# Attention with routed experts on one core: weighted sum ten steps behind the scores, routing rounds of 24 tiles, key chunks loaded two in turn

## The chip, the cores and the metric

The kernel runs on one core of a Trainium2 chip. The metric is the device time of one execution in microseconds (us); lower is better. A core has five engines with an instruction stream each: TensorE (PE in the profile; its weight loads are PEld), VectorE (DVE), ScalarE (ACT), GpSimd (POOL) and SyncE (SP, which here only issues DMAs). Each stream is executed in order and waits on semaphores. SP and POOL both issue DMAs; POOL also computes.

## The reference

Four batches of pooled attention, then a mixture of experts over all 49,152 output rows:

```python
def _attn_ref(q, kv, w_sr):                       # q (4, 12288, 128), kv (4, 384, 32, 128)
    kv_pool = kv.reshape(B, H // 4, 4, W // 4, 4, C).mean(axis=(2, 4))
    k = v = kv_pool.reshape(B, -1, C) @ w_sr      # 768 keys a batch
    s = (q @ k.transpose(0, 2, 1)) / sqrt(C)
    a = exp(s - s.max(-1)); a /= a.sum(-1) + 1e-09
    return a @ v

def _moe_ref(x, w_skip, w_gate, w1, w2):          # 8 experts, 128 -> 1024 -> 128
    act = x @ w_skip > 0                          # rows that are computed
    e = argmax(x @ w_gate); g = softmax(x @ w_gate)[e]
    out[act] = x + g * (relu(x @ w1[e]) @ w2[e])  # the others keep x
```

## The kernel before

The attention phase works on 384 tiles of 128 queries, 96 to a batch. A loop over steps t writes all engines' streams by hand; a step takes one tile through one stage each of a pipeline. In step t, `scores(t)` issues six 384-column matmuls (query in a high and a low part, keys too), `row_max(t)` reduces them on DVE (L641), `row_exp(t)` is the exponential on ACT (L646). One step later `p_hi` (ACT, L650) and `p_lo` (DVE, L654) split four of the six key chunks of the weights into two f16 parts, which SP sends through a transposing DMA into `pt` (L657). The other two chunks are transposed on PE two steps later (`p_transpose`, L670) and split from PSUM (L678, L679). `attend(t - LAG)` with LAG = 8 is the weighted sum, 18 matmuls of 138 columns (L696). Four tiles form a group; queries come a group at a time (`load_q`, three groups ahead), their high part is cast on ACT (L612), their low part is subtracted on POOL in two halves (L615, `q_lo`), placed in the steps t + 2 and t + 4 after a group's second step, two groups before use.

The keys and values of the next batch arrive during the current one: six chunks of four row sets each. The first row set of a chunk is a plain DMA from SP (L444), the other three are DMAs from POOL that add into the same tile (L446); each must wait until the one before it has landed. `KV_T` places one of the 24 loads every 3.25 steps, chunk after chunk. POOL then folds the chunk (L472, L475) four steps after its last load.

Routing: every RT = 12 tiles, when the last of them is summed, a job `route(r, ...)` starts. It yields between its parts, so that they spread over the next twelve steps: gate logits and maximum on DVE (L741, L743), five elementwise operations on POOL (L745 to L759), one-hot marks (L771 to L774), a scan that ranks the rows of each expert (L779), three tiny matmuls over the partitions (L793 to L795), destinations (L799 to L822), and `send_rows`. That one reads a flag on POOL and, inside a `tc.If`, scatters the rows into a DRAM buffer `scr` with one indirect DMA (L191). The job for round r ends in the step in which that of round r + 1 begins, and stands just ahead of it in POOL's stream.

The last 60 steps also load and split the weights and rows of one expert group whose place is known after three batches. From step 384 on, PE does what is left of the weighted sums interleaved with this first group (`peel`), DVE works out the last round and a table of all groups (`make_table`), and then the expert loop starts: 17 passes over 2,048 rows, bound by PE, which the change doesn't touch.

Of the kernel before, what the change touches and what calls it, by code (L numbers as in the profile page):

```python
# [9 lines left out]
F32 = mybir.dt.float32  # L10
F32R = mybir.dt.float32r
BF16 = mybir.dt.bfloat16
# [8 lines left out]
RT = 12  # L21
# [3 lines left out]
def kernel(  # L25
# [33 lines left out]
    RG = RT // GT  # L59
    TPB = NQ // P  # L60
# [3 lines left out]
    LAG = 8  # L64
    TLAG = 2
    W1, W2, W3 = 3, 6, 0
# [46 lines left out]
    idt_i = consts.tile([P, RT], I32, name="idt_i")  # L113
    nc.gpsimd.iota(idt_i, pattern=[[1, RT]], base=BIG, channel_multiplier=RT)
    idt = consts.tile([P, RT], F32, name="idt")
    nc.gpsimd.tensor_copy(idt, idt_i)

    marks = [consts.tile([P, E, RT + 1], F16, name=f"marks{i}") for i in range(3)]
    for x in marks:
        nc.gpsimd.memset(x, 0.0)  # L120
    keep = consts.tile([P, E, RT + 1], F32, name="keep")
# [282 lines left out]
    with ExitStack() as p1:  # L404
        kprep = p1.enter_context(tc.tile_pool(name="kprep", bufs=1))
        kvm = p1.enter_context(tc.tile_pool(name="kvm", bufs=2))
        qp = p1.enter_context(tc.tile_pool(name="qp", bufs=4))
        qt = p1.enter_context(tc.tile_pool(name="qt", bufs=3))
# [192 lines left out]
        LASTR = NTILE // RT - 1  # L601
        SNAPR = LASTR - 8

# [80 lines left out]
        def attend(t):  # L684
# [23 lines left out]
            def scale():  # L708
# [13 lines left out]
        def route(r, eng):  # L722
            rows = ROWS[r]
            S3 = [P, RT, E]
            x_sc = KV[r * RT // TPB][5]

            def small_t(name, dt=F32):
                return rt.tile([P, RT], dt, name=name)

            def big_t(name, dt=F32):  # L730
                return rt.tile([P, RT, E], dt, name=name)
# [6 lines left out]
            def em(x):  # L738
                return x.unsqueeze(1).broadcast_to(S3)
# [21 lines left out]
            ohb = mark.rearrange("p e t -> p t e")[:, 1:RT + 1, :]  # L761
            yield
            fast = r >= LASTR - 1
# [5 lines left out]
            nc.scalar.copy(rows[:, :, C + 2], x_sc.broadcast_to([P, RT]))  # L769
# [7 lines left out]
            inner = rt.tile([P, E, RT + 1], BF16, name="inner")  # L777
# [4 lines left out]
            nc.vector.tensor_reduce(out=full, in_=inner[:, :, RT], axis=AX.X, op=ALU.max)  # L782
            odd = rt.tile([P, 1], BF16, name="odd")
            nc.vector.scalar_tensor_tensor(out=odd, in0=full, scalar=float(RT), in1=full, op0=ALU.subtract, op1=ALU.mult)
# [8 lines left out]
            nc.tensor.matmul(ps[:, 0:E], upper_bf, inner[:, :, RT], start=True, stop=True)  # L793
            nc.tensor.matmul(ps[:, E:2 * E], ones_bf, inner[:, :, RT], start=True, stop=True)
# [11 lines left out]
            eng.tensor_tensor(out=acc, in0=inner.rearrange("p e t -> p t e")[:, 0:RT, :], in1=em(carry[:, 0, :]), op=ALU.add)  # L806
            eng.tensor_tensor(out=acc, in0=acc, in1=ohb, op=ALU.mult)
            eng.tensor_scalar(out=gs, in0=gs, scalar1=1e-9, scalar2=x_sc, op0=ALU.add, op1=ALU.mult)
            nc.gpsimd.iota(rows.bitcast(I32)[:, :, C + 1], pattern=[[1, RT]], base=r * RT * P, channel_multiplier=RT)
# [4 lines left out]
            if r == SNAPR:  # L814
# [6 lines left out]
            bi = rt.tile([P, 1], I32, name="bi")  # L821
            nc.vector.scalar_tensor_tensor(out=bi, in0=rows.bitcast(I32)[:, 0, C + 1:C + 2], scalar=float(TRASH),  # L822
                                           in1=di[:, 0:1], op0=ALU.add, op1=ALU.min)
            if not few:
                yield
            send_rows(rows, di, bi, mixed)
# [135 lines left out]
        ptq = p1.enter_context(tc.tile_pool(name="ptq", bufs=5))  # L962
        hl = p1.enter_context(tc.tile_pool(name="hl", bufs=6))
# [6 lines left out]
        for i in range(KC * R):  # L970
            KV_T.setdefault(i * 13 // 4, []).append(divmod(i, R))
# [6 lines left out]
        while t < NTILE + LAG - 1 or next_l or jobs:  # L978
# [45 lines left out]
            if t == NTILE:  # L1024
                p_s.close()
                p_kv.close()
                alloc_h(p1.enter_context(tc.tile_pool(name="hp1", bufs=1)))
# [93 lines left out]
```

## Time and profile before

| what | value |
|---|---|
| time, median of 3 runs | 1790.56 us (1790.5 to 1798.45) |
| time of the profiled execution | 1793.98 us |
| its span, first to last instruction | 1792.2 us |
| PE busy | 97% |
| DVE busy | 86% |
| ACT busy | 74% |
| POOL busy | 37% |
| mean granted TensorE clock | 0.996 of full speed |

The busy shares are of the whole span: some 950 us of attention and routing, where four engines work, and some 740 us of the expert loop, where PE is alone the bound. A busy PE need not be at its peak, since a matmul's recorded time covers its passage through the pipeline; the distance from the start of one matmul to the start of the next tells the pace.

### The profile page before, as it was taken

What the parts mean: (1) busy time and instruction counts of PE and PEld (TensorE: products, weight loads), DVE (VectorE), ACT (ScalarE), POOL (GpSimd) and SP (SyncE); (2) the same over time, 40 slices, a digit from 0 to 9 for tenths busy, and PEclk for the clock granted to TensorE, in tenths of its full rate; (3) what the DMA queues carried; (4) which work ended last, traced back from release to release, by engine and by line L of the source; (5) the groups of instructions that cost most, each with busy time, mean ns of one, the idle gap of its engine ahead of it and who ended that gap; (6) DMA issues with size and microseconds to landing.
All of it is one profiled execution on the core that took longest, in us unless ns stands there. A gap on an engine that the chain in (4) does not pass through costs nothing. (4 is left out here: it accounts for less than half of the span.)

```text
span 1792.2 us, 42121 instructions
## 1 busy us (share of the span) xinstructions
PE 1731.6 (97%) x13954; PEld 1248.1 (70%) x13954; DVE 1539.2 (86%) x3405; ACT 1318.1 (74%) x2519; POOL 666.5 (37%) x959
## 2 busy tenths in 40 slices
PE   3999999999999999999999999999999999999997
PEld 2899999989899898999989544444444444444443
DVE  6899999999899898999999778878888887788886
ACT  2888888888888887889899456666666666666664
POOL 3334433443443444233323233333333333333334
PEclk9999999999999999999999999999999999999999
DMA  7999999999999999999999333343333333333333
GB/s 180 193 215 224 219 226 205 217 224 216 218 199 213 221 211 214 187 184 202 241 185 209 102 85 100 98 102 95 95 95 98 102 97 102 97 95 104 99 101 84
DMA packets 609814, 284.84 MB, mean 159 GB/s; under 512 B 495616, under 2 KB 564352, under 8 KB 609664
## 3 DMA queue, kind: packets, MB, share of 16 engines
q1 hardware_dynamic: 588064, 222.76, 63.0%
q0 software_dynamic: 21600, 60.19, 13.0%
q8 instruction: 82, 1.34, 0.3%
q14 instruction: 68, 0.56, 0.1%
HBM read 90.47 MB, written 72.30 MB: 91 GB/s over the span
## 5 line engine op out<-in xcount | busy, mean ns | idle before, releaser
L183 POOL DMA_INDIRECT out_dram<-o,ids x288 | 283.3, 984 | 486.8 <-DVE o L325 419.0
L294 DVE SCALAR_TENSOR_TENSOR h_lo<-h_ps,h_hi 128x512 f16<-128x512 f32 x544 | 343.9, 685 | 134.2 <-ACT h_hi L293 134.2
L646 ACT ACTIVATE p_sb<-s_ps,nm 128x768 f32<-128x768 f32 x384 | 347.3, 905 | 126.5 <-DVE nm L641 123.5
L641 DVE TENSOR_REDUCE nm<-s_ps 128x1 f32<-128x768 f32 x384 | 364.7, 950 | 34.0 <-PE s_ps L635 32.4
L293 ACT ACTIVATE h_hi<-h_ps 128x512 f16<-128x512 f32 x544 | 317.9, 597 | 46.9 <-PE h_ps L292 27.3
L696 PE MATMUL acc_ps<-v_hi,pt 128*128 128x138 f16 x3072 | 320.9, 224 | 0.8 <-DVE rs L704 0.7
L696 PEld LDWEIGHTS <-pt 128*128 128x128 f16 x4608 | 275.9, 97 | 62.0 <-issue 60.3
L696 PE MATMUL acc_ps<-v_lo,pt 128*128 128x138 f16 x1536 | 293.5, 223 | 0.0
L633 PE MATMUL s_ps<-k_hi,q_hi 128*128 128x384 f32 x768 | 292.3, 381 | 0.0
L654 DVE SCALAR_TENSOR_TENSOR p<-p_sb,p 128x512 f16<-128x512 f32 x384 | 282.8, 736 | 3.9 <-ACT p L650 3.9
L635 PE MATMUL s_ps<-k_hi,q_lo 128*128 128x384 f32 x768 | 260.5, 339 | 8.1 <-POOL q_lo L615 8.1
L634 PE MATMUL s_ps<-k_lo,q_hi 128*128 128x384 f32 x768 | 260.8, 340 | 0.0
L650 ACT ACTIVATE p<-p_sb 128x512 f16<-128x512 f32 x384 | 243.3, 634 | 3.6 <-DMA pt<-p 0.8
L615 POOL TENSOR_TENSOR q_lo<-q_sb,q_hi 128x256 fp32r<-128x256 f32 (+1 forms) x190 | 154.2, 820 | 186.2 <-DVE p L654 115.7
L290 PE MATMUL h_ps<-xT,w_hi 128*128 128x512 f16 x544 | 206.2, 379 | 2.5 <-issue 2.5
L306 PEld LDWEIGHTS <-w_hi 128*128 128x128 f16 x1152 | 112.7, 98 | 134.2 <-issue 0.8
L306 PE MATMUL y_ps<-h_hi,w_hi 128*128 128x512 f16 x544 | 206.2, 379 | 0.0
L306 PE MATMUL y_ps<-h_hi,w_lo 128*128 128x512 f16 x544 | 206.2, 379 | 0.0
L291 PE MATMUL h_ps<-xT,w_hi 128*128 128x512 f16 x544 | 206.2, 379 | 0.0
L292 PE MATMUL h_ps<-xT,w_lo 128*128 128x512 f16 x544 | 206.2, 379 | 0.0
L309 ACT ACTIVATE yT<-y_ps,y_sc 128x512 f32<-128x512 f32 x68 | 46.7, 687 | 214.7 <-PE y_ps L306 155.7
L306 PE MATMUL y_ps<-h_lo,w_hi 128*128 128x512 f16 x544 | 195.1, 379 | 0.0
(214 smaller groups left out, 3039.7 us busy)
## 6 DMA issues: line engine op xcount, KB each, us to landing
q_sb<-in_q_dram SPq DMA_DIRECT2D x96, 256.0 KB
out_dram<-rows SPq DMA_DIRECT2D x96, 256.0 KB
xin<-scr SPq DMA_DIRECT2D x75, 276.0 KB
w_raw<-in_moe_w_dram SPq DMA_DIRECT2D x34, 512.0 KB, 3.4
kvt<-in_kv_dram POOLq DMA_DIRECT2D x54, 256.0 KB
kvt<-in_kv_dram SPq DMA_DIRECT2D x42, 256.0 KB
pt<-p SPq DMA_TRANSPOSE x384
out_dram<-o,ids POOLq DMA_INDIRECT x288, 3.6
```

Source lines behind the costliest of these rows:

```text
L183: ins = nc.gpsimd.indirect_dma_start(out=dst, out_offset=bass.IndirectOffsetOnAxis(ap=ids, axis=0), in_=src, in_offset=None, bounds_check= ...
L293: nc.scalar.activation(out=h["hi"][:, c, :], in_=ps, func=AF.Relu)
L294: nc.vector.scalar_tensor_tensor(out=h["lo"][:, c, :], in0=ps, scalar=0.0, in1=h["hi"][:, c, :], op0=ALU.max, op1=ALU.subtract)
L306: nc.tensor.matmul(ps, w[:, c, :], h[x][:, c, :], start=(i == 0), stop=(i == len(terms) - 1))
L633: nc.tensor.matmul(s[:, h, :HK], q_hi, k_hi[:, sl], start=True, stop=False)
L634: nc.tensor.matmul(s[:, h, :HK], q_hi, k_lo[:, sl], start=False, stop=False)
L635: nc.tensor.matmul(s[:, h, :HK], q_lo, k_hi[:, sl], start=False, stop=True)
L641: nc.vector.tensor_reduce(out=NM[t], in_=S_PS[t][:, :, :HK], axis=AX.XY, op=ALU.max, negate=True)
L646: nc.scalar.activation(out=P_SB[t], in_=S_PS.pop(t)[:, :, :HK], func=AF.Exp, bias=NM.pop(t))
L650: nc.scalar.activation(out=P16[t][:, 0, :], in_=p_flat(t)[:, 0:KD * P], func=AF.Copy, scale=2.0 ** PEXP)
L654: LO[:] = [nc.vector.scalar_tensor_tensor(out=p16[:, 1, :], in0=p_flat(t)[:, 0:KD * P], scalar=2.0 ** PEXP, in1=p16[:, 0, :], op0=ALU.mult ...
L696: nc.tensor.matmul(ps[:, j % 2, :], w, v[a][:, k, :], start=(i == 0), stop=(i == len(AVL) - 1))
```

## The change

Five edits, made together:

- LAG goes from 8 to 10: `attend` works on the tile ten steps back. The buffers between (`pt`, `ptq`, and `hl` for the split weights, 6 to 9) grow with it.
- Routing rounds hold NB = 2 blocks of 12 tiles, so RQ = 24. All tiles of `route` are twice as wide, there are 16 rounds and not 32, and each round sends its two blocks separately, six steps apart. In the last round they go back to back. `rowp` and `rt` have two buffers and not three.
- `KV_T` pairs the chunks: the first row set of chunk a, then of chunk b, then the second of a, the second of b, and so on. The 24 loads keep their steps.
- Queries load four groups ahead and not three.
- The pooled chunks and their transposed copy lie in the expert weights' raw buffers `w1_raw` and `w2_raw`, which are first loaded later. This frees room.

```diff
-    LAG = 8
+    NB = 2
+    RQ = NB * RT
+    LAG = 10
+    QA = 4
...
-        rt = p1.enter_context(tc.tile_pool(name="rt", bufs=3))
+        rt = p1.enter_context(tc.tile_pool(name="rt", bufs=2))
...
-                pooled[b] = kprep.tile([P, KC, C], F32, name="pooled")
+                pooled[b] = w1_raw[:, 0:NK].rearrange("p (k c) -> p k c", c=C)
...
-                KVT[b] = kprep.tile([P, NK], F32, name="pT")
+                KVT[b] = w2_raw.rearrange("p k c -> p (k c)")[:, 0:NK]
...
-        LASTR = NTILE // RT - 1
-        SNAPR = LASTR - 8
+        LASTR = NTILE // RQ - 1
+        SNAPR = LASTR - 4
...
-                if o == 0:
-                    ROWS[r] = rowp.tile([P, RT, XW], F32, name="rows")
-            rows = ROWS[r][:, o * GT:(o + 1) * GT, :]
+                if o == 0 and r % NB == 0:
+                    ROWS[r // NB] = rowp.tile([P, RQ, XW], F32, name="rows", bufs=2)
+            at = r % NB * RT + o * GT
+            rows = ROWS[r // NB][:, at:at + GT, :]
...
-                if o == RG - 1:
-                    jobs.append([route(r, nc.vector if r == LASTR else nc.gpsimd), None])
+                if o == RG - 1 and r % NB == NB - 1:
+                    jobs.append([route(r // NB, nc.vector if r // NB == LASTR else nc.gpsimd), None])
...
-            S3 = [P, RT, E]
+            S3 = [P, RQ, E]
...
-            fast = r >= LASTR - 1
+            fast = few
...
-            send_rows(rows, di, bi, mixed)
+            for h in range(NB):
+                part = slice(h * RT, (h + 1) * RT)
+                send_rows(rows[:, part, :], di[:, part], bi[:, h:h + 1], mixed)
+                if h < NB - 1 and not few:
+                    for _ in range(6):
+                        yield
...
-        ptq = p1.enter_context(tc.tile_pool(name="ptq", bufs=5))
-        hl = p1.enter_context(tc.tile_pool(name="hl", bufs=6))
+        ptq = p1.enter_context(tc.tile_pool(name="ptq", bufs=6))
+        hl = p1.enter_context(tc.tile_pool(name="hl", bufs=9))
...
         for i in range(KC * R):
-            KV_T.setdefault(i * 13 // 4, []).append(divmod(i, R))
+            two, at = divmod(i, 2 * R)
+            KV_T.setdefault(i * 13 // 4, []).append((2 * two + at % 2, at // 2))
...
-                if t % GT == 0 and t // GT + RG < NGRP:
-                    load_q(t // GT + RG)
+                if t % GT == 0:
+                    for g in range(3 if t == 0 else t // GT + QA, min(t // GT + QA + 1, NGRP)):
+                        load_q(g)
```

Place one is POOL's stream where a block of rows is sent in the attention phase. Before, the scatter (`scr<-rows,bi`; the twelve single scatters behind it are the branch not taken) is followed at once by the five operations of the next round:

```order
L1117 ISA
L191 DMA scr<-rows,bi 460800x138
L190 ISA
L190 UNCONDITIONAL_BRANCH
L183 DMA scr<-rows,di 460800x138 x12
L190 UNCONDITIONAL_BRANCH
L745 TENSOR_TENSOR d<-lg,mx 128x96
L756 TENSOR_SCALAR ev<-d 128x96
L757 TENSOR_TENSOR ev<-ev,em_80 128x96
L758 TENSOR_SCALAR act<-rows 128x12
L759 TENSOR_SCALAR na<-act 128x12
L615 TENSOR_TENSOR q_lo<-q_sb,q_hi 128x256 x2
```

After the change (line numbers are a few higher) the same place, a round's second block:

```order
L1131 ISA
L194 DMA scr<-rows,bi 460800x138
L193 ISA
L193 UNCONDITIONAL_BRANCH
L186 DMA scr<-rows,di 460800x138 x12
L193 UNCONDITIONAL_BRANCH
L619 TENSOR_TENSOR q_lo<-q_sb,q_hi 128x256 x2
L450 DMA kvt<-in_kv_dram 128x1x512
L750 TENSOR_TENSOR d<-lg,mx 128x192
```

The query halves now stand directly behind the scatter, and the next round's operations, twice as wide, come four steps later.

Place two is POOL's stream during the accumulation of key chunks, with buffer numbers kept, since they tell the chunks apart. Before, one chunk (`kvt_790`) has its three adding loads in a row:

```order
L446 DMA kvt_790<-in_kv_dram 128x1x512
L615 TENSOR_TENSOR q_lo_793<-q_sb_571,q_hi_792 128x256
L615 TENSOR_TENSOR q_lo_969<-q_sb_745,q_hi_968 128x256
L446 DMA kvt_790<-in_kv_dram 128x1x512
L745 TENSOR_TENSOR d_1104<-lg_1100,mx_1102 128x96
L756 TENSOR_SCALAR ev_1106<-d_1104 128x96
L757 TENSOR_TENSOR ev_1106<-ev_1106,em8_80 128x96
L758 TENSOR_SCALAR act_1107<-rows_561 128x12
L759 TENSOR_SCALAR na_1108<-act_1107 128x12
L615 TENSOR_TENSOR q_lo_969<-q_sb_745,q_hi_968 128x256
L446 DMA kvt_790<-in_kv_dram 128x1x512
```

After, two chunks (`kvt_356` and `kvt_443`) alternate:

```order
L450 DMA kvt_356<-in_kv_dram 128x1x512
L619 TENSOR_TENSOR q_lo_750<-q_sb_464,q_hi_749 128x256
L450 DMA kvt_443<-in_kv_dram 128x1x512
L619 TENSOR_TENSOR q_lo_750<-q_sb_464,q_hi_749 128x256
L619 TENSOR_TENSOR q_lo_923<-q_sb_552,q_hi_922 128x256
L450 DMA kvt_356<-in_kv_dram 128x1x512
L619 TENSOR_TENSOR q_lo_923<-q_sb_552,q_hi_922 128x256
L450 DMA kvt_443<-in_kv_dram 128x1x512
```

Between two loads into the same chunk there are now six or seven steps, where there were three or four.

Place three is DVE's stream in the last routing round, beside the first expert group (`h_lo` is that group's second operand, `o` its output). Before:

```order
L325 SCALAR_TENSOR_TENSOR o<-acc_ps,xin_135 128x128 x4
L741 TENSOR_TENSOR lg<-rows,gate_ds 128x96
L743 TENSOR_REDUCE mx<-lg 128x12
L745 TENSOR_TENSOR d<-lg,mx 128x96
L751 SCALAR_TENSOR_TENSOR ev<-d,em_80 128x96
L752 TENSOR_SCALAR act<-rows 128x12
L753 SCALAR_TENSOR_TENSOR na<-rows,idt 128x12
L294 SCALAR_TENSOR_TENSOR h_lo<-up_ps,h_hi 128x512 x2
L771 TENSOR_REDUCE mn<-ev 128x12
L773 TENSOR_TENSOR oh<-em_80,mn 128x96
L774 TENSOR_TENSOR marks_89<-oh,act 128x12x8
L294 SCALAR_TENSOR_TENSOR h_lo<-up_ps,h_hi 128x512 x2
```

After:

```order
L297 SCALAR_TENSOR_TENSOR h_lo<-up_ps,h_hi 128x512 x2
L746 TENSOR_TENSOR lg<-rows,gate_ds 128x192
L748 TENSOR_REDUCE mx<-lg 128x24
L750 TENSOR_TENSOR d<-lg,mx 128x192
L756 SCALAR_TENSOR_TENSOR ev<-d,em_80 128x192
L757 TENSOR_SCALAR act<-rows 128x24
L758 SCALAR_TENSOR_TENSOR na<-rows,idt 128x24
L776 TENSOR_REDUCE mn<-ev 128x24
L778 TENSOR_TENSOR oh<-em_80,mn 128x192
L779 TENSOR_TENSOR marks_88<-oh,act 128x24x8
L784 SCALAR_TENSOR_TENSOR inner<-keep,marks_88 128x200
L787 TENSOR_REDUCE full<-inner 128x1
```

The round's operations now follow each other without the group's operations in between, since PE is in a part of the group that makes no `h_lo`; on PE the three routing matmuls now stand behind a whole second half of the group (24 matmuls into the output and 12 of the next) after the last weighted sum, and the table comes later in the group.

## Rows read from the trace of the kernel before

**Rows 1.** Windows view, attention phase: time, busy time of each engine (instructions), clock
```profile
50.00:350.00 300.00, 297.62 (x3235) 276.42 (x3236) 274.66 (x569) 257.77 (x484) 121.20 (x201) 1.00 1.14 215
```

**Rows 2.** Timeline of PE: first score matmul of tiles two apart
```profile
301.19 0.42 PE L633 MATMUL s_ps<-k_hi,q_hi 128*128 128x384 f32 x1
...
305.94 0.42 PE L633 MATMUL s_ps<-k_hi,q_hi 128*128 128x384 f32 x1
```

**Rows 3.** Timeline of ACT: exponentials of tile 8 and of tile 383
```profile
54.70 0.90 ACT L646 ACTIVATE p_sb<-s_ps,nm 128x768 f32<-128x768 f32 x1 [0.44 <-DVE nm L641]
...
985.29 0.90 ACT L646 ACTIVATE p_sb<-s_ps,nm 128x768 f32<-128x768 f32 x1
```

**Rows 4.** Groups by form, 50 to 1000 us: largest of the preparation's matmuls, busy us
```profile
L558 PE MATMUL acc_ps<-wv,pT 128*128 128x138 f32 x36 | 5.6, 292 | 0.4 <-DVE rs L704 0.2
```

**Rows 5.** View of waits, 50 to 1000 us: total us, times, longest
```profile
POOL kvt L446 <- DMA kvt<-in_kv_dram: 72.4, 18, 6.3
...
DVE mn L771 <- POOL ev L757: 13.4, 7, 4.5
...
PEld acc_ps L670 <- ACT p_sb L646: 9.5, 24, 0.9
PEld s_ps L635 <- POOL q_lo L615: 9.3, 4, 3.7
...
ACT q_hi L612 <- DMA q_sb<-in_q_dram: 5.3, 5, 2.1
```

**Rows 6.** Timeline of POOL around the longest of those waits of PE
```profile
682.77 0.86 POOL L446 DMA_DIRECT2D kvt<-in_kv_dram  x1 [4.85 <-DVE nm L641]
685.00 1.09 POOL L191 DMA_INDIRECT scr<-rows,bi  x1 [1.37 <-DVE rs L704]
690.35 0.34 POOL L745 TENSOR_TENSOR d<-lg,mx 128x96 f32<-128x96 f32 x1 [4.27 <-DMA kvt<-in_kv_dram]
```

**Rows 7.** Timeline of PE and windows view at the same place
```profile
693.07 0.69 PE L635 MATMUL s_ps<-k_hi,q_lo 128*128 128x384 f32 x1 [3.40 <-POOL q_lo L615]
...
693.20:696.20 3.00, 3.00 (x19) 2.69 (x20) 2.96 (x6) 2.47 (x5) 2.46 (x4) 0.50 1.11 248
```

**Rows 8.** Timeline of POOL: a scatter with no key load in flight
```profile
978.84 1.58 POOL L191 DMA_INDIRECT scr<-rows,bi  x1 [4.27 <-DVE bi L822]
980.45 0.36 POOL L745 TENSOR_TENSOR d<-lg,mx 128x96 f32<-128x96 f32 x1
```

**Rows 9.** Instructions of line 190 on POOL's sequencer: ns least/median/most
```profile
L190 POOLq EVENT_SEMAPHORE  x96: 42/43/3068, 113.2 to 1018.3; - x96
```

**Rows 10.** Groups by form of DVE, 50 to 1000 us: busy us, mean ns
```profile
L641 DVE TENSOR_REDUCE nm<-s_ps 128x1 f32<-128x768 f32 x378 | 359.0, 950 | 33.9 <-PE s_ps L635 32.4 <-issue 0.2
...
L779 DVE TENSOR_TENSOR_SCAN inner<-keep,marks 128x104 bf16<-128x104 f32 x31 | 13.2, 427 | 1.5 <-POOL marks L774 1.5
...
L743 DVE TENSOR_REDUCE mx<-lg 128x12 f32<-128x96 f32 x31 | 7.8, 253 | 1.1
...
L802 DVE TENSOR_SCALAR mixed<-acc_ps 1x1 int32<-1x1 f32 x31 | 4.2, 136 | 0.0
```

**Rows 11.** Instructions of line 654 on DVE: ns least/median/most
```profile
L654 DVE SCALAR_TENSOR_TENSOR p<-p_sb,p x384: 670/690/2225, 39.5 to 987.2; 128x512 f16<-128x512 f32 x192
```

**Rows 12.** Timeline of PE: two steps before the first weighted sum
```profile
50.02 0.44 PE L670 MATMUL acc_ps<-ident,p_sb 128*128 128x128 f32 x2 [0.30 <-ACT p_sb L646]
...
51.85 0.33 PE L670 MATMUL acc_ps<-ident,p_sb 128*128 128x128 f32 x1 [0.33 <-ACT p_sb L646]
```

**Rows 13.** Timeline of PE: waits between the last scores and the expert loop
```profile
1014.92 0.18 PE L793 MATMUL acc_ps<-inner,upper_bf 128*128 128x8 bf16 x1 [1.80 <-DVE inner L779]
...
1029.09 0.38 PE L306 MATMUL acc_ps<-h_lo,w_hi 128*128 128x512 f16 x1 [0.49 <-DVE h_lo L294]
1030.97 0.58 PE L306 MATMUL acc_ps<-h_lo,w_hi 128*128 128x512 f16 x1 [1.50 <-DVE h_lo L294]
```

More of the change, by code (lines that the diff above doesn't have):

```diff
@@ L112 @@
                             op0=ALU.mult, op1=ALU.add)
-    idt_i = consts.tile([P, RT], I32, name="idt_i")
-    nc.gpsimd.iota(idt_i, pattern=[[1, RT]], base=BIG, channel_multiplier=RT)
-    idt = consts.tile([P, RT], F32, name="idt")
+    idt_i = consts.tile([P, RQ], I32, name="idt_i")
+    nc.gpsimd.iota(idt_i, pattern=[[1, RQ]], base=BIG, channel_multiplier=RQ)
+    idt = consts.tile([P, RQ], F32, name="idt")
     nc.gpsimd.tensor_copy(idt, idt_i)
-    marks = [consts.tile([P, E, RT + 1], F16, name=f"marks{i}") for i in range(3)]
+    marks = [consts.tile([P, E, RQ + 1], F16, name=f"marks{i}") for i in range(3)]
     for x in marks:
         nc.gpsimd.memset(x, 0.0)
-    keep = consts.tile([P, E, RT + 1], F32, name="keep")
+    keep = consts.tile([P, E, RQ + 1], F32, name="keep")
     nc.gpsimd.memset(keep, 1.0)
@@ L768, in route @@
             nc.scalar.activation(out=ex, in_=d, func=AF.Exp)
-            nc.scalar.copy(rows[:, :, C + 2], x_sc.broadcast_to([P, RT]))
+            nc.scalar.copy(rows[:, :, C + 2], x_sc.broadcast_to([P, RQ]))
             mn = small_t("mn")
@@ L776, in route @@
                 yield
-            inner = rt.tile([P, E, RT + 1], BF16, name="inner")
+            inner = rt.tile([P, E, RQ + 1], BF16, name="inner")
             flat = "p e t -> p (e t)"
@@ L781, in route @@
             full = rt.tile([P, 1], F32, name="full")
-            nc.vector.tensor_reduce(out=full, in_=inner[:, :, RT], axis=AX.X, op=ALU.max)
+            nc.vector.tensor_reduce(out=full, in_=inner[:, :, RQ], axis=AX.X, op=ALU.max)
             odd = rt.tile([P, 1], BF16, name="odd")
-            nc.vector.scalar_tensor_tensor(out=odd, in0=full, scalar=float(RT), in1=full, op0=ALU.subtract, op1=ALU.mult)
+            nc.vector.scalar_tensor_tensor(out=odd, in0=full, scalar=float(RQ), in1=full, op0=ALU.subtract, op1=ALU.mult)
             gs = small_t("gs")
@@ L792, in route @@
             ps = misc_ps()
-            nc.tensor.matmul(ps[:, 0:E], upper_bf, inner[:, :, RT], start=True, stop=True)
-            nc.tensor.matmul(ps[:, E:2 * E], ones_bf, inner[:, :, RT], start=True, stop=True)
+            nc.tensor.matmul(ps[:, 0:E], upper_bf, inner[:, :, RQ], start=True, stop=True)
+            nc.tensor.matmul(ps[:, E:2 * E], ones_bf, inner[:, :, RQ], start=True, stop=True)
             nc.tensor.matmul(ps[:, 2 * E:2 * E + 1], ones_bf, odd, start=True, stop=True)
@@ L805, in route @@
             acc = big_t("acc")
-            eng.tensor_tensor(out=acc, in0=inner.rearrange("p e t -> p t e")[:, 0:RT, :], in1=em(carry[:, 0, :]), op=ALU.add)
+            eng.tensor_tensor(out=acc, in0=inner.rearrange("p e t -> p t e")[:, 0:RQ, :], in1=em(carry[:, 0, :]), op=ALU.add)
             eng.tensor_tensor(out=acc, in0=acc, in1=ohb, op=ALU.mult)
             eng.tensor_scalar(out=gs, in0=gs, scalar1=1e-9, scalar2=x_sc, op0=ALU.add, op1=ALU.mult)
-            nc.gpsimd.iota(rows.bitcast(I32)[:, :, C + 1], pattern=[[1, RT]], base=r * RT * P, channel_multiplier=RT)
+            nc.gpsimd.iota(rows.bitcast(I32)[:, :, C + 1].rearrange("p (b t) -> p b t", b=NB),
+                           pattern=[[RT * P, NB], [1, RT]], base=r * RQ * P, channel_multiplier=RT)
             yield
@@ L820, in route @@
             nc.vector.tensor_tensor(out=di, in0=dest, in1=na, op=ALU.add)
-            bi = rt.tile([P, 1], I32, name="bi")
-            nc.vector.scalar_tensor_tensor(out=bi, in0=rows.bitcast(I32)[:, 0, C + 1:C + 2], scalar=float(TRASH),
-                                           in1=di[:, 0:1], op0=ALU.add, op1=ALU.min)
+            bi = rt.tile([P, NB], I32, name="bi")
+            nc.vector.scalar_tensor_tensor(out=bi, in0=rows.bitcast(I32)[:, 0:RQ:RT, C + 1], scalar=float(TRASH),
+                                           in1=di[:, 0:RQ:RT], op0=ALU.add, op1=ALU.min)
             if not few:
                 yield
-            send_rows(rows, di, bi, mixed)
+            for h in range(NB):
[4 more added lines that the diff above has]
+                        yield
             if r == SNAPR:
@@ L1026 @@
                 p_kv.close()
+                p_q.close()
                 alloc_h(p1.enter_context(tc.tile_pool(name="hp1", bufs=1)))
```

13 lines of the change are left out of this document (7 added, 6 removed).

## The prediction

> **What bounds the kernel now.** The windows view of the attention phase comes first: in 300 us PE is busy for 297.6, but DVE for 274.7 and ACT for 257.8 too [rows 1]. So PE leads, and DVE is close behind; what costs time are the moments in which PE waits for one of the others. How much that is in all follows from the pace. In a quiet stretch two tiles take 305.94 - 301.19 = 4.75 us on PE, 2.375 a tile [rows 2]. From tile 8 to tile 383 ACT's exponentials go from 54.70 to 985.29, 930.6 us for 375 tiles [rows 3]; at the quiet pace they would need 890.6. The excess is 40 us. Not all of it is waiting: the keys and values of three batches are prepared on PE, and the largest of four kinds of matmuls for it is 5.6 us [rows 4], so that all together are 6 to 22, and three small matmuls stand in each routing round. Some 15 to 30 us of stalls are left, and that is the ceiling for this phase. The expert loop behind it is untouched.
>
> The view of waits names two causes, read on PEld, since a matmul that waits first holds up its weight load: 9.3 us in 4 times for `q_lo` from POOL, and 9.5 us in 24 times for the exponentials of ACT [rows 5]. The first has a clear story in POOL's timeline. At 682.77 POOL issues an adding load, then the scatter at 685.00, and it gets to the next round's first operation only at 690.35, released by the load's landing [rows 6]: 7.6 us from the load. On POOL's sequencer the waits around the scatter's branch are mostly 43 ns, but up to 3068 [rows 9], and with no load in flight POOL is through in 980.45 - 978.84 = 1.6 us [rows 8]. So the end of that branch waits for key loads still in flight. Then came five routing operations, then `q_lo`, and PE stood for 3.40 us; the clock granted after that was 0.50, that is 1.2 GHz and not 2.4 [rows 7].
>
> **The change, part by part.**
>
> *Key chunks in turn.* The load ahead of the scatter was itself late: 18 times, one for each chunk of three batches, an adding load waited for the one before it, 72.4 us in all and up to 6.3 [rows 5]. Two loads into one chunk now stand six or seven steps apart (14 us and more at 2.375) and not three or four (7 to 9.5). A load needs less than the 7.6 us of [rows 6], so it has landed. Then POOL reaches scatters on time, and behind the scatter stands `q_lo` at once. Loads and scatters still meet in one step twice a batch (steps 6 and 48, from the 3.25-step grid and the rounds' start). There POOL is held for 7.6 us, 3.2 steps, and a half of `q_lo` that is placed one step behind is needed five steps behind; about one step is left over. I take -9 us; bounds -9.3, and +4 if each of the six meetings cost 0.7, a quarter of the cover that I count on.
>
> *The clock.* The stretch at half clock behind the 3.40 us wait gave 19 matmuls in 3 us [rows 7]; half of its length was lost. It goes with the wait: -1.5 us; bounds 0 and -2.
>
> *Rounds of 24 on DVE.* Fourteen DVE operations a round, from 427 to 136 ns, make 3.36 us in 12 tiles. Twice the width costs little: 96 elements take 253 ns and 768 take 950, a slope of 1.04 ns an element [rows 10]; seven operations are 96 elements wide, so a round of 24 costs 3.36 + 7 x 0.10 and 0.1 more for the scan, 4.2 us, where two of before cost 6.7. That frees 2.5 us of DVE in 24 tiles, 39 us in the phase, 4% of an engine 92% busy. It isn't a gain by itself, since PE leads; it shortens the lag that makes exponentials late. Two other sources of the lag go: DVE waited 13.4 us for POOL's `ev`, behind the scatter [rows 5], which now has four free steps ahead of it; and ACT waited 5.3 us for queries [rows 5], which now come one group (9.5 us) sooner. Against the 9.5 us of [rows 5] I take -7; bounds 0 and -9.5.
>
> *Rounds of 24 on PE and POOL.* Fifteen sets of three small matmuls fewer in the phase, and short waits that no row names one by one: -3 us out of the unnamed rest of the 15 to 30; bounds 0 and -6. Scatters stay 32, and so do their branches. POOL's operations get longer, but are half as many; POOL is busy 121 of 300 us [rows 1].
>
> *LAG 10.* The weighted sums don't wait for their transposed weights before, so the longer lag saves nothing there. It costs at the start: two more steps without a weighted sum. Such a step takes 51.85 - 50.02 = 1.83 us with 0.30 to 0.33 idle by the record [rows 12]; its matmuls alone are 2.375 less 18 of some 0.06, 1.3 us. Two steps lose 0.6 to 1.1 us, and the sums moved to the end are paid in full there: +1.
>
> *The end.* Before, PE waited 1.80 us for the last round and 0.49 + 1.50 for `h_lo` behind the table [rows 13]. After, 36 matmuls stand between the last weighted sum and the routing matmuls; they are recorded at 0.38 us and overlap [rows 13], so that 36 make 6.8 us even at half of that, and DVE's chain of eleven operations of 0.25 to 0.45 is done in 5. That wait goes, -2. But the table now comes later in the group, with fifteen of its operations ahead of one `h_lo`; +2. I take 0; bounds -4 and +4.
>
> *Buffers in the weights' place, two `rows` buffers.* The weights are first loaded 34 steps after the last use of the keys there: nothing. `rows` is the first rival below.
>
> Sum: -9 - 1.5 - 7 - 3 + 1 + 0 = -19.5 us. All gains at their bound: -9.3 - 2 - 9.5 - 6 + 0.6 - 4 = -30. The profiled execution took 1793.98 us, its span 1792.2; the median of the runs is 1790.56, 3.4 less. The profiled time would be 1774.5, and the median 1771.
>
> **The rivals.**
>
> *Slower: `rows` is reused too soon.* With two buffers of 24 tiles, the second scatter of a round is placed six steps ahead of ACT's first write into the same buffer; before it was 26. Six steps are 14.2 us. If POOL reaches the scatter late and the transfer lasts long, ACT waits, and the exponentials behind it. It decides once scatter and landing need more than 14.2 us from that step; POOL's hold of 7.6 us [rows 6] plus a transfer like it would be 15. Each of 14 rounds would then lose a step or so, 14 x 2.4 = 33 us, less the gains of 19.5: 1804. Against it: the second scatter waits for nothing of DVE that isn't long done, and only that of step 6, three times in all, meets a load. Chance 0.07.
>
> *Same: PE's own pace.* If the late exponentials come from the even and odd steps of the pipeline itself and not from routing, the relief on DVE stays unused, and longer single operations (0.35 for 0.25 us) push ACT as often as before. Then only the wait for `q_lo`, the clock, and +1 count, and a part of -9 comes back as waits for ACT: -5 us, 1785. The 24 waits on ACT, nearly one for each of 31 rounds, speak for routing as the cause. Chance 0.17.
>
> *Longer POOL operations hold up DVE.* Line 654 takes 690 ns mostly and 2225 at most [rows 11], the long ones while POOL computes. POOL's routing operations nearly double; if each collision costs twice as much, the relief on DVE is eaten, -7 becomes about 0 or +2, and the time 1779. By the Trainium skill (SBUF — State Buffer, "Who interferes with whom") the second of a VectorE instruction with two SBUF inputs and a GpSimd instruction that reads SBUF blocks until the first has ended, so a longer operation blocks longer; the 2225 ns of line 654 agree. Chance 0.10.
>
> *The change doesn't do what it says.* If the adding loads wait for their turn in the queue and not for the landing of the one before, the turn-taking is void and the wait for `q_lo` stays: -19.5 + 10.5 = -9, 1781.5. The row names the landing as what ended the waits. Chance 0.06.
>
> **How the numbers follow.** The forecast has 0.60: 1771, by its own bounds 1761 to 1780. A measurement here tells 0.5% from no change, 9 us, so faster means below 1781.6. The forecast, the collisions and half of the void turn-taking lie below: 0.60 + 0.10 + 0.03 = 0.73. Within 0.5%: 0.17 + 0.03 = 0.20. Slower: 0.07. The range leaves out the slower rival and the tail of the forecast: 1760 to 1787.
>
> **What the profile would show.** Right: the wait of POOL's adding loads falls from 72.4 us to under 20, PE's wait for `q_lo` from 9.3 to under 2, no half clock inside the attention phase; DVE's routing rows number 15 with 4.2 us a round; PE's wait for exponentials is under 4 us; tile 383's exponential comes 18 to 20 us sooner. Wrong: ACT waits for a scatter's landing ahead of its write into `rows`; PE waits for `q_lo` behind steps 6 and 48; PE waits for ACT as often as before though DVE is less busy; or the expert loop starts later than the attention phase's gain allows.

## The result, and the profile after

| | before | changed | ratio [95% interval] |
|---|---|---|---|
| first comparison, median of 6 and 6 runs | 1793.18 us | 1772.44 us (1770.70 to 1778.48) | 0.9866 [0.9833, 0.9899] |
| the same kernel again, on another chip, 26 and 6 runs | 1799.62 us | 1782.01 us (1774.99 to 1785.26) | 0.9910 [0.9874, 0.9945] |
| profiled execution, span | 1792.2 us | 1776.7 us | |

The changed kernel is faster by 0.9 to 1.3% by the two ratios, and by 21 and 18 us by the medians; 19.5 was forecast. The second comparison was made beside the last experiments. The two ratios differ by 0.0044, 8 us, so a variant within that of the changed kernel isn't told apart from it below. The execution profiled first (1778.48 us) was the slowest of its six.

The gain lies where it was expected, in the attention phase. The timeline of ACT after the change, exponentials of tile 8 and tile 383:

```profile
54.59 0.90 ACT L650 ACTIVATE p_sb<-s_ps,nm 128x768 f32<-128x768 f32 x1 [0.44 <-DVE nm L645]
...
966.23 0.90 ACT L650 ACTIVATE p_sb<-s_ps,nm 128x768 f32<-128x768 f32 x1 [0.31 <-DVE nm L645]
```

Against [rows 3] tile 383 is 985.29 - 966.23 = 19.06 us sooner, and tile 8 stands where it stood. What follows tile 383 takes 3.6 us more (1776.7 - 966.2 = 810.5, before 1792.2 - 985.3 = 806.9). In the changed kernel's second profile the same instruction stands at

```profile
960.91 0.90 ACT L650 ACTIVATE p_sb<-s_ps,nm 128x768 f32<-128x768 f32 x1 [0.31 <-DVE nm L645]
```

5.3 us sooner still, though tile 8 stands 1.7 us later there (56.29). So one profile places this mark within some 5 us; the experiments' differences of that size mean nothing by themselves.

Nor does this mark alone say when the expert loop starts. PE's first matmul of the loop, in the first and in the second profile of the changed kernel:

```profile
1028.32 0.58 PE L293 MATMUL h_ps<-xT,w_hi 128*128 128x512 f16 x1 [2.68 <-issue]
...
1028.61 0.59 PE L293 MATMUL h_ps<-xT,w_hi 128*128 128x512 f16 x1 [8.24 <-issue]
```

The second profile gained 5.3 us up to the mark and lost them again ahead of the loop, where PE stood 8.24 us (2.49 in the kernel before). What holds the loop's start there no row tells.

The windows view of the stretch of [rows 1] (time, then PE, PEld, DVE, ACT, POOL busy with their instructions, clock, DMA share, GB/s):

```profile
50.00:350.00 300.00, 297.20 (x3224) 275.90 (x3225) 264.32 (x504) 260.96 (x480) 109.92 (x153) 1.00 1.17 216
```

DVE is 10.3 us less busy in 300 us and POOL 11.3, while PE remains as full as it was. Why DVE is freed is read from the groups by form, 50 to 1000 us (busy us, mean ns of one, idle before):

```profile
L658 DVE SCALAR_TENSOR_TENSOR p<-p_sb,p 128x512 f16<-128x512 f32 x379 | 270.3, 713 | 3.0 <-ACT p L654 2.7 <-ACT p_sb L650 0.3
...
L784 DVE TENSOR_TENSOR_SCAN inner<-keep,marks 128x200 bf16<-128x200 f32 x16 | 9.1, 568 | 0.0
...
L748 DVE TENSOR_REDUCE mx<-lg 128x24 f32<-128x192 f32 x16 | 5.6, 353 | 0.5
...
L807 DVE TENSOR_SCALAR mixed<-acc_ps 1x1 int32<-1x1 f32 x15 | 2.0, 136 | 0.0
```

`mx` went from 253 to 353 ns at twice the width, the scan from 427 to 568, a scalar operation stayed at 136 [rows 10]. The fourteen means of a round add up to 4.08 us, where 4.2 was forecast. The split of the weights (L658) takes 713 ns on the mean; before it was 279.4 us over 379 operations, 737 ns.

The view of waits, 50 to 1000 us (who waited on whom: total us, times, longest), against [rows 5]:

```profile
POOL kvt L450 <- DMA kvt<-in_kv_dram: 31.6, 8, 10.7
...
POOL scr L194 <- DMA kvt<-in_kv_dram: 15.8, 10, 2.3
...
PEld L700 <- DMA pt<-p: 9.5, 21, 1.9
...
PEld acc_ps L674 <- ACT p_sb L650: 7.4, 14, 1.0
ACT p L654 <- DMA pt<-p: 7.3, 6, 1.8
```

The adding loads wait 31.6 us and not 72.4 (23.1 in the second profile). PE's wait for `q_lo` is gone, and so are DVE's for `ev` and ACT's for queries. What is new is the third row: PE waits for `pt`, the weights that come back through SP's transposing DMA, and ACT too waits for it, to have a buffer free.

How that wait arises is seen in the timeline of SP's sequencer (start, duration of the issue; a row with x3 runs from the first issue's start to the third's end):

```profile
436.53 1.24 SPq L661 DMA_TRANSPOSE pt<-p  x1
...
438.49 7.53 SPq L661 DMA_TRANSPOSE pt<-p  x3
...
450.93 10.20 SPq L661 DMA_TRANSPOSE pt<-p  x3
```

and, 5 us behind the last of these, in PE's:

```profile
456.37 0.29 PE L700 MATMUL acc_ps<-v_hi,pt 128*128 128x138 f16 x2 [1.60 <-DMA pt<-p]
```

The first issue takes 1.24 us. The three from 438.49 on take 1.29, 4.56 and 1.47, the three from 450.93 on 3.40, 3.38 and 3.21, where key loads (issued by POOL at 438.12 and 447.48) and scatters (441.23 and 453.97) are in flight, so that SP falls behind its steps of 2.4 us. By the Trainium skill (DMA: Bandwidth & Descriptors, "Queues, rings and completion order") each DMA engine goes round-robin between the queue rows with work, a packet at a time; that a transpose is slower while POOL's transfers run agrees with these rows, though they show its issue and not its packets.

A late SP also holds up POOL. SP issues the first row set of a chunk (L448), and POOL's first adding load waits for it; here are SP's rows and then POOL's:

```profile
397.26 8.36 SPq L661 DMA_TRANSPOSE pt<-p  x3
...
406.34 0.60 SPq L448 DMA_DIRECT2D kvt<-in_kv_dram  x1
...
412.67 0.99 POOL L450 DMA_DIRECT2D kvt<-in_kv_dram  x1 [10.72 <-DMA kvt<-in_kv_dram]
```

All eight waits that make up the 31.6 us are of this kind: each ends with the landing of a load that SP issued, none with that of another adding load. Before, too, 11 of the 18 waits, 44.7 of the 72.4 us, ended with a load of SP's.

### The profile page after: what moved, and what is told of

Read it like the earlier page. It is cut to its first block, busy times and chain, and to the rows that moved or that the text cites. A ratio compares the mean times of both kernels' runs of the same rounds, so it can differ in the third digit from the quotient of the medians.

```text
span 1776.7 us, 41426 instructions
## 1 busy us (share of the span) xinstructions
PE 1721.4 (97%) x13906; PEld 1240.2 (70%) x13906; DVE 1502.7 (85%) x3181; ACT 1317.0 (74%) x2487; POOL 632.0 (36%) x799
## 3 DMA queue, kind: packets, MB, share of 16 engines
q0 software_dynamic: 21600, 60.19, 12.9%
## 5 line engine op out<-in xcount | busy, mean ns | idle before, releaser
L658 DVE SCALAR_TENSOR_TENSOR p<-p_sb,p 128x512 f16<-128x512 f32 x384 | 273.7, 713 | 3.0 <-ACT p L654 2.7
L619 POOL TENSOR_TENSOR q_lo<-q_sb,q_hi 128x256 fp32r<-128x256 f32 (+1 forms) x190 | 147.8, 779 | 327.2 <-DVE p L658 195.6
```

Source lines behind the costliest of these rows:

```text
L658: LO[:] = [nc.vector.scalar_tensor_tensor(out=p16[:, 1, :], in0=p_flat(t)[:, 0:KD * P], scalar=2.0 ** PEXP, in1=p16[:, 0, :], op0=ALU.mult ...
```

## The experiments

All ratios are to the kernel before, run beside it on the same chip, with their 95% intervals. "PE stands" means the sum, over PE's matmuls of the phase, of what the distance from one start to the next has over the median distance of that kind of pair; for the kernel before it gives 10.5 us at `q_lo` and 8.2 us ahead of the transposes by PE, where the exponentials are waited for. The changed kernel has 6.4 for `pt` and 4.6 for the exponentials.

**Key chunks in turn, alone.** The kernel before with only the new `KV_T`:

```diff
-            KV_T.setdefault(i * 13 // 4, []).append(divmod(i, R))
+            two, at = divmod(i, 2 * R)
+            KV_T.setdefault(i * 13 // 4, []).append((2 * two + at % 2, at // 2))
```

> The kernel before with the key chunks two in turn and nothing else changed. Theory (turn-taking alone ends the wait for q_lo and the half clock that follows it): PE's wait for q_lo falls from 9.3 to under 2 us and the time falls by 9 to 11 us, to about 1783 (0.994). Rival (the scatter and the five operations behind it hold up the query halves whatever the loads do): PE's wait for q_lo stays above 5 us and the time stays at 1790 to 1793 (0.998 to 1.000).

Measured: 1798.77 us, 1.0025 [0.9994, 1.0056]. No gain. The view of waits, 50 to 1000 us:

```profile
ACT q_hi L612 <- DMA q_sb<-in_q_dram: 22.8, 17, 3.4
PEld acc_ps L670 <- ACT p_sb L646: 17.2, 24, 2.8
ACT p L650 <- DMA pt<-p: 16.7, 9, 4.6
...
PEld L696 <- DMA pt<-p: 5.8, 5, 2.8
```

Neither the adding loads' wait nor PE's for `q_lo` has a row any more, so the edit does what the prediction said, and yet nothing is won: ACT waits 22.8 us for queries (5.3 before) and 16.7 for the buffers of its split weights, and PE waits for ACT 17.2 us where it was 9.5. The stall changed its place.

**Chunks in a row again.** The changed kernel with the old `KV_T`, `divmod(i, R)`:

> The changed kernel with the key chunks loaded one after the other, as before. Theory (turn-taking ends the late adding loads, which held up the scatter and the query halves): POOL's wait of adding loads on the landing of the one before goes back to about 70 us, PE's wait for q_lo back to 5 us or more, and the time rises by 5 to 11 us, to about 1780 (0.992). Rival (the wait for q_lo went since the next round's operations no longer stand behind the scatter): PE's wait for q_lo stays under 2 us and the time stays at about 1772.

Measured: 1779.00 us, 0.9897 [0.9860, 0.9934], not told apart from the changed kernel. Its waits:

```profile
POOL kvt L450 <- DMA kvt<-in_kv_dram: 128.6, 31, 9.0
...
PEld acc_ps L674 <- ACT p_sb L650: 17.5, 21, 2.9
...
ACT rows L716 <- DMA scr<-rows,bi: 3.6, 1, 3.6
...
PEld s_ps L639 <- POOL q_lo L619: 0.2, 1, 0.2
```

The adding loads wait 128.6 us, more than ever, and PE still doesn't wait for `q_lo`. So the late loads are not enough for that stall: in the kernel before, five routing operations stood between the scatter and `q_lo`; here `q_lo` stands directly behind the scatter. The third row is the first rival's wait, a write into `rows` held by a scatter: once, 3.6 us.

**LAG 10 alone.** The kernel before with the longer lag and buffers for it:

```diff
-    LAG = 8
+    LAG = 10
...
-        ptq = p1.enter_context(tc.tile_pool(name="ptq", bufs=5))
-        hl = p1.enter_context(tc.tile_pool(name="hl", bufs=6))
+        ptq = p1.enter_context(tc.tile_pool(name="ptq", bufs=6))
+        hl = p1.enter_context(tc.tile_pool(name="hl", bufs=8))
```

> The kernel before with the weighted sum ten steps behind and the buffers that go with it (6 for the PE-transposed chunks, 8 for the split weights), no other edit. Theory (before, PE hardly waits for transposed weights; it does so only where POOL and DVE no longer slow the phase down, so the lag is worth something only together with the other edits): the time stays within 0.3% of before, ratio 0.998 to 1.002, PE's wait for q_lo stays near 9 us. Rival (the lag by itself is worth the 15 us that the changed kernel lost with eight): ratio about 0.992.

Measured: 1793.78 us, 0.9974 [0.9946, 1.0002]: at most half a per cent. Its waits:

```profile
POOL kvt L446 <- DMA kvt<-in_kv_dram: 101.2, 27, 7.2
...
PEld acc_ps L670 <- ACT p_sb L646: 16.3, 22, 2.6
```

No row of PE names `q_lo`. A round starts when its last tile is summed, so LAG moves every scatter by two steps against loads and queries; in this profile all but two of the scatters are followed by `q_lo`. So the stall at `q_lo` needed two things, a late load and the five operations between scatter and `q_lo`: the chunks in turn take away the first, the wide rounds and LAG 10 the second. Here too PE waits for ACT instead, 16.3 us for 9.5.

**LAG 8 in the changed kernel.**

```diff
-    LAG = 10
+    LAG = 8
```

> The changed kernel with the weighted sum eight steps behind and not ten, all else as changed. Theory (the lag saves nothing by itself and costs 1 us at the start): the time stays within 0.3% of the changed kernel, about 1771 us (ratio to before 0.986), and PE waits for transposed weights about as much as with ten, 5 to 10 us. Rival (SP's queue falls behind when a key load and a scatter meet, and the two extra steps of lag cover that): PE's waits for transposed weights rise by 10 us or more, and the time to about 1780 us (0.992).

Measured: 1788.45 us, 0.9951 [0.9922, 0.9979]; against the changed kernel that is 7 to 15 us, by which of its two comparisons one takes. Its waits:

```profile
PEld L700 <- DMA pt<-p: 19.8, 15, 3.6
PE acc_ps L700 <- DMA pt<-p: 15.1, 12, 3.3
...
PEld acc_ps L674 <- ACT p_sb L650: 3.7, 8, 1.1
```

PE stands 18.6 us for `pt`, and waits only 3.7 for ACT. So the two steps are cover: with ten, the transposed weights are late by 6.4 us in one profile and by nothing that can be told in the other (no single wait above 0.2); with eight, by 18.6.

**Queries three groups ahead in the changed kernel.**

```diff
-    QA = 4
+    QA = 3
```

> The changed kernel with queries loaded three groups ahead, as before, and not four. Theory (with turn-taking alone ACT waited 22.8 us for queries, since DMAs land later; the group ahead covers that): ACT's wait for queries comes back with 5 us or more, and the time rises by 2 to 6 us (ratio 0.988 to 0.990). Rival (the other edits cover it): no wait of ACT for queries, and the time stays at 0.9866.

Measured: 1787.02 us, 0.9947 [0.9915, 0.9979], 7 to 14 us above the changed kernel. Its waits:

```profile
ACT q_hi L616 <- DMA q_sb<-in_q_dram: 35.3, 26, 3.8
...
PEld acc_ps L674 <- ACT p_sb L650: 21.7, 25, 2.6
```

ACT waits 26 times for queries, as often as PE then waits for ACT: 25 times, 19.5 us by PE's starts. A late query is a late exponential.

**Queries four ahead, alone.** The kernel before with that edit and a fifth query buffer:

```diff
-                if t % GT == 0 and t // GT + RG < NGRP:
-                    load_q(t // GT + RG)
+                if t % GT == 0:
+                    for g in range(3 if t == 0 else t // GT + 4, min(t // GT + 5, NGRP)):
+                        load_q(g)
```

> The kernel before with queries four groups ahead and not three, and nothing else. If queries pay by themselves, ACT's wait for queries (5.3 us before) goes to 0 and the ratio is 0.992 to 0.996. If they pay only where something else has moved the DMAs into their way, as with three groups in the changed kernel (35 us of waits), nothing is gained: ratio 0.998 to 1.002, and PE keeps its wait of about 10 us for q_lo.

Measured: 1797.87 us, 0.9980 [0.9949, 1.0011]. ACT's wait for queries is gone, and the time stays. Its waits:

```profile
PEld s_ps L635 <- POOL q_lo L615: 11.4, 5, 5.7
...
PEld acc_ps L670 <- ACT p_sb L646: 5.6, 16, 0.9
```

PE waits less for ACT (5.6 for 9.5), and as long as before for `q_lo`, to which nothing was done.

**The cover alone.** The changed kernel with rounds of 12 and chunks in a row; what is left is LAG 10, queries four ahead, nine split-weight buffers:

```diff
-    NB = 2
+    NB = 1
...
-        SNAPR = LASTR - 4
+        SNAPR = LASTR - 8
...
-            two, at = divmod(i, 2 * R)
-            KV_T.setdefault(i * 13 // 4, []).append((2 * two + at % 2, at // 2))
+            KV_T.setdefault(i * 13 // 4, []).append(divmod(i, R))
```

(`rt` and `rows` have three buffers again.)

> The changed kernel without its two edits that were meant to help POOL and DVE: key chunks in a row as before, rounds of 12. What is left is LAG 10, queries four groups ahead, and nine buffers for the split weights. If the gain comes from cover for late DMAs, most of it stays: 1775 to 1784 us (ratio 0.988 to 0.993), and PE waits for exponentials and transposed weights stay under 20 us together. If chunks in turn and wide rounds are what gives the gain, as the prediction had it (16.5 of 19.5 us), the time goes back to about 1790 to 1797 (ratio 0.995 to 1.0), with an adding-load wait of POOL above 70 us and a wait of PE for q_lo.

Measured: 1793.04 us, 0.9976 [0.9949, 1.0002]. The first expectation falls: cover alone gives half a per cent at most. Its waits:

```profile
POOL kvt L450 <- DMA kvt<-in_kv_dram: 108.4, 27, 8.0
...
PEld acc_ps L674 <- ACT p_sb L650: 16.2, 20, 3.4
...
PEld L700 <- DMA pt<-p: 3.2, 20, 0.2
```

The second expectation named the time rightly, but not by its wait: of `q_lo` PE has one wait of 0.7 us; it waits for ACT.

**Rounds of 12 in the changed kernel.** As above, but with the chunks in turn:

> The changed kernel with routing rounds of 12 tiles (32 rounds, three buffers of rows and of the routing tiles), all else as changed. Theory (half the rounds free about 39 us of DVE, which is what ended the late exponentials): DVE is busy some 30 to 40 us more between 50 and 1000 us, PE waits for exponentials about 9 us again, and the time is 7 to 10 us above the changed kernel, about 1780 (0.992). Rival (DVE's slack is enough either way): the time stays within 3 us of the changed kernel.

Measured: 1782.94 us, 0.9913 [0.9882, 0.9944]. Beside the cover alone this adds the chunks in turn: 0.9976 becomes 0.9913. Beside the changed kernel it lacks the wide rounds, which are worth 0 to 8 us by the two comparisons. Its waits:

```profile
PEld L700 <- DMA pt<-p: 11.2, 26, 1.4
...
PEld acc_ps L674 <- ACT p_sb L650: 8.1, 15, 1.4
```

DVE is busy for 867.3 us between 50 and 1000 us, against 845.5 in the changed kernel: 22 us more, where 30 to 40 were expected. And PE waits 8.1 us for the exponentials, against 7.4 and 6.4 in the two profiles of the changed kernel: hardly more, though the routing takes DVE twice as many rounds.

**Six split-weight buffers in the changed kernel** (`hl` 9 to 6):

> The changed kernel with six buffers for the split weights and not nine. Theory (these buffers come free when the transposing DMA has read them; turn-taking alone made ACT wait 16.7 us for that): ACT's wait for transposing DMAs rises from 7 to 15 us or more, PE waits for exponentials more, and the time rises by 3 to 8 us (0.988 to 0.991). Rival (six are enough at this pace): time within 2 us of the changed kernel.

Measured: 1780.40 us, 0.9899 [0.9865, 0.9932], not told apart. The wait that the buffers cover is there all the same:

```profile
ACT p L654 <- DMA pt<-p: 34.5, 27, 3.8
...
PEld acc_ps L674 <- ACT p_sb L650: 15.1, 21, 2.1
```

**Loads moved out of the scatters' steps.** The changed kernel with another grid:

```diff
-            KV_T.setdefault(i * 13 // 4, []).append((2 * two + at % 2, at // 2))
+            KV_T.setdefault(24 * two + (2, 7, 9, 11, 14, 16, 18, 20)[at], []).append((2 * two + at % 2, at // 2))
```

> The changed kernel with the 24 key loads of a batch on steps that keep clear of the scatters (eight per 24 steps, none in a scatter's step or the two ahead of it), still two chunks in turn. Theory (transposed weights are late where key loads and scatters are in flight together, around 445 to 460 us in the changed kernel): PE's and ACT's waits for transposing DMAs fall from 17 to under 6 us together, POOL no longer waits for a key load at a scatter, and the time falls by 3 to 6 us (0.983 to 0.985). Rival (the transposes are late by their own number, whatever POOL's DMAs do): waits for transposing DMAs stay above 10 us and the time stays at 0.9866.

Measured: 1772.04 us, 0.9849 [0.9811, 0.9888], within the intervals of the changed kernel. No scatter has a key load within 8 us ahead of it any more, where the first profile of the changed kernel has twelve (counted in POOL's timeline). Its waits:

```profile
POOL kvt L450 <- DMA kvt<-in_kv_dram: 53.8, 19, 6.7
...
PEld L700 <- DMA pt<-p: 13.5, 20, 2.3
...
ACT p L654 <- DMA pt<-p: 8.3, 8, 1.7
```

The theory expected the waits of PE and ACT for transposes to fall from 17 to under 6 us; they are 21.8. So its rival came out: the transposes are late though no load and scatter meet, and the time stays. Two things weaken the comparison. The profile is of the slowest of this kernel's seven executions (1785.85 us). And the new grid puts loads into one chunk four to seven steps apart and not six or seven, so that adding loads wait for each other again (10 of the 19 waits). POOL is held less behind its scatters, and PE doesn't gain by it.

**The same with queries five groups ahead** (QA 5, `hl` 8):

> The changed kernel with the loads' steps moved off those of the scatters, queries five groups ahead and eight buffers for split weights. If queries are still late now and then, another 2 to 5 us are gained over the changed kernel: 1767 to 1770, ratio 0.983 to 0.985. If four groups are enough, the time is that of the run with the loads moved alone, ratio 0.985 to 0.987, or a little above for the buffer that is missing.

Measured: 1785.77 us, 0.9934 [0.9901, 0.9968]. No further gain; it may even cost something, for which its waits give only a part (ACT for `pt` 18.3 us in 11 times, PE for ACT 11.7).

**The changed kernel again.**

> The changed kernel once more, beside the others of this call: ratio 0.984 to 0.989. Its profile tells how far tile 383's exponential (966.2 us in the first profile) and the single waits move from one execution to the next: by under 3 us if the differences between the other profiles are to be read at face value, by 5 us and more if not.

Measured: 1782.01 us, 0.9910 [0.9874, 0.9945], the second line of the first table; its mark is 5.3 us off that of the first profile. PE's wait for `pt` is 1.7 us in 11 times, against 9.5 us in 21.

## Why the prediction was right, and which steps were not

The time, 1771, came out, in the phase that was forecast and with most of the waits that were to go. That the sum came out so closely is luck in part: of its terms, one was set at nothing that wasn't, two were smaller than forecast, and over a quarter of the gain between the marks has no name. PE's time between the two exponentials, added up by line from the starts of its matmuls (a wait counts with the line ahead of it), went from 930.6 to 911.6 us: scores 439.1 to 431.8, weighted sums 421.4 to 413.1, transposes 54.9 to 53.6, routing matmuls 3.2 to 1.2. Term by term:

- **Wait for `q_lo`:** -10.5 by the starts, -9 forecast. The wait went. But the step that gave the whole of it to the chunks in turn was wrong: it goes too with chunks in a row and wider rounds (adding loads waiting 128.6 us), and with LAG 10 alone (101.2 us), where something else stands between scatter and `q_lo`. "An adding load waited for the one before it" was read too narrowly: 11 of the 18 waits were for SP's plain load. Of such waits 31.6 and 23.1 us remain, over the 20 that were named as a sign. And the step that the wait's end is a gain of its own was wrong as well: the chunks in turn alone remove it and measure 1.0025 [0.9994, 1.0056].
- **The branch that waits for loads in flight:** right. In the kernel before 16 of 30 scatters had an adding load issued within 8 us ahead and held POOL 4.2 us on the mean, the other 14 1.6 us. "Twice a batch" was too few: four meet in a batch. The longest hold after is 5.6 us, and behind it `q_lo` is still on time, so the cover that the prediction counted on was there.
- **Clock:** -1.7 for -1.5, half of the 3.4 us at half clock behind [rows 7]. They are gone in the first profile; the second has 3.4 us, but at 49 us, before the first weighted sums.
- **DVE:** a round costs 4.08 us (4.2 forecast), and PE stands 6.2 us ahead of and within the transposes where it was 10.7, -4.5 for -7. The target of under 4 us in the view of waits was missed (7.4 from 9.5). That the 4.5 us come from DVE's relief is not shown: with rounds of 12 PE waits 8.1 us there, not much longer than the changed kernel, and queries four ahead alone bring 9.5 to 5.6. Queries belong to a term of their own: in the changed kernel three groups instead of four cost 7 to 14 us, far over the 5.3 us of [rows 5].
- **Routing on PE:** -2.0 for -3.
- **LAG 10, "saves nothing there":** the failed step. The weighted sums did not wait for transposed weights before, but they would after: with eight steps PE stands 18.6 us for `pt`. The term was read from a trace in which, as it seems, other waits had slowed the tiles and so covered the DMAs; SP, whose DMAs these are, had no term at all. Of this new wait 6.4 us remain in the first profile and next to nothing in the second; no term had it.
- **The end:** 3.6 us longer, forecast +1 for the moved sums and 0 for the rest. Two tiles' sums more are done behind the mark (180 matmuls for 144; 36 of 0.06, 2.2 us), and one fewer between the marks (6732 for 6750, -1.1): +1.1 in all, as forecast. Half clock lasts 6.8 us from 1026.6 where it lasted 3.4 from 1031.0, which costs half of the difference, 1.7. That makes 3.9 for 3.6. In the second profile the end is 8.4 us longer than before (815.3 for 806.9), 5.8 of them in PE's longer stand ahead of the loop. So the sign that the loop starts later than the phase's gain allows did show there, and its cause stays open.

Between the marks these terms together are -10.5 - 4.5 - 2.0 - 1.7 - 1.1 + 6.4 = -13.4 of the -19.0; the other 5.6 are spread over many small distances, and their cause is left open.

Of the rivals, the reuse of `rows` has no row in the changed kernel and one of 3.6 us with chunks in a row. Longer POOL operations did not hold DVE longer: L658 has 713 ns on the mean for 737, with the same extremes as in [rows 11] to 12 ns. The Trainium skill (SBUF — State Buffer, "Who interferes with whom") lets one of two colliding instructions block until the other has ended; the trace before agrees with that, since all 24 of these operations that took over 900 ns overlap an operation of POOL. But 23 of the 24 overlap `q_lo` and not routing; in the changed kernel 15 of 22 do, and 5 stand beside the wide routing operations. Nor do fewer routing operations explain the drop: the mean is 712 ns with the turns alone, 705 in the changed kernel with rounds of 12, and 749 with wide rounds and chunks in a row. "PE's own pace" would have left DVE's relief unused; as the effect of that relief on PE isn't shown, this rival isn't ruled out for the wide rounds.

What the runs show is that the gain of the turns isn't one to be added: alone they measure 1.0025, while on top of the cover they bring 0.9976 to 0.9913. LAG alone (0.9974) and queries alone (0.9980) are worth half a per cent at most, and so is the cover together (0.9976). Cover with either relief is worth 0.9 to 1.0% (0.9913 with the turns, 0.9897 with the wide rounds), and all five 0.9 to 1.3%. Wide rounds alone, and turns and wide rounds without cover, were not run, so whether the wide rounds would pay by themselves stays open.

A fifth engine belongs in the account. SP does nothing but issue DMAs, and between the two exponentials it spends nearly as much of its time on that as DVE on computing. The table gives this share, the mean time of one transposing issue, and how long after the end of `p_lo`, when its data are there, the issue starts (all added up in the traces):

| kernel | SP's share | one issue | behind its data, mean and longest |
|---|---|---|---|
| before | 86.5% | 1.69 us | 2.4 and 8.0 us |
| turns alone | 87.1% | 1.72 us | 2.9 and 10.0 us |
| cover alone | 86.5% | 1.68 us | 2.3 and 11.4 us |
| changed, chunks in a row | 88.4% | 1.74 us | 3.3 and 11.5 us |
| changed, rounds of 12 | 88.5% | 1.73 us | 5.7 and 16.2 us |
| changed, loads moved | 88.7% | 1.73 us | 5.8 and 17.4 us |
| changed, two profiles | 89.8%, 89.3% | 1.73, 1.70 us | 5.8 and 18.1, 4.4 and 12.9 us |

The reading that fits these rows: the phase is a ring of engines at nearly one pace, SP among them. As POOL and DVE are relieved, tiles come faster, SP has less time left over, and its transposes and queries start later behind their data; with cover for those alone, POOL's and DVE's lateness still reaches PE through the exponentials. An issue is longer while POOL's DMAs are in flight, before the change as after it: in the changed kernel 1.42 us on the mean with no key load and no scatter in flight, 1.95 with a load, 2.09 with a scatter, 2.39 with both, and before 1.43, 1.85, 1.84 and 2.46 (taking 5.8 us for a load and 6.6 for a scatter where the landing wasn't recorded, the medians of those that were). That key loads on time are what makes SP late is argued: in three pairs of kernels the turns raise SP's lateness (2.4 to 2.9, 2.3 to 5.7, 3.3 to 5.8 and 4.4), but one issue is hardly longer for them, and keeping loads and scatters apart doesn't lower it. No run gave SP less to do, so that SP is what comes next is read from these rows and not tested.

## What to carry to other kernels

Where several engines and queues run at nearly one pace, don't price an edit by the wait that it removes: ask which wait of similar size stands right behind, and give that its cover (lag, earlier loads, buffers) in the same change. "X doesn't wait for Y now" says nothing on whether it will once the others are faster, so a longer lag or an earlier load should not be set at zero from a trace of the slower kernel. Count the engine that only issues DMAs like any other: here SP was busy for 86 to 90% of the phase. And test edits both ways, alone and taken out of the whole: here LAG and the queries are worth 0.3% or less alone and 0.4 to 0.8% when they are taken out.

## What was unexpected in the hardware

- Issuing a transposing DMA from SP takes 1.24 us in quiet stretches and 3.2 to 3.4 us in a stretch where POOL's adding loads and scatters are in flight (three in 10.20 us); the longest in the phase took 5.07 us. So the issuing engine, not only the landing, falls behind.
- The end of a conditional block on POOL waited up to 3.07 us for key loads in flight in the kernel before [rows 9], and up to 3.95 us after the change, as the row of its sequencer shows:

```profile
L193 POOLq EVENT_SEMAPHORE  x96: 42/43/3953, 148.9 to 1011.5; - x96
```

- DVE's routing operations over all experts take 1.2 to 1.5 times as long at twice the width (`mx` 253 to 353 ns from 96 to 192 elements, `dest` 197 to 298), so about half of a small operation or more doesn't depend on its width.
